# A key stage whose LayerNorm rows are made one tile earlier and partly turned by DMAs

## The chip, the cores and the metric

The kernel runs on one core of a Trainium2 chip. The time is that of one launch in device microseconds; of several runs the median is given. A core has five engines that work beside each other, each through its own list of instructions in order: TensorE (PE, with its weight loads PEld), VectorE (DVE), ScalarE (ACT), GpSimd (POOL) and SyncE (SP). In this kernel SP only issues DMAs. Engines wait for each other through semaphores.

## What is computed

The program is the forward and the backward pass of four residual blocks over 2048 rows of 512 numbers in bf16: attention, feed-forward, attention, feed-forward, with weights shared by the two blocks of a kind. Each block works on the LayerNorm of its input (mean taken off, divided by the standard deviation, no gain):

```python
x = x + _A_ref(_layernorm(x), A_wqkv, A_wo)
x = x + _B_ref(_layernorm(x), B_w_gate, B_w_up, B_w_down)
x = x + _A_ref(_layernorm(x), A_wqkv, A_wo)
x = x + _B_ref(_layernorm(x), B_w_gate, B_w_up, B_w_down)
```

`_A_ref` is linear attention with 32 heads of 16: q, k, v = x @ wqkv; phi(t) = (t + 1 if t > 0 else exp(t)) + 1e-6 is applied to q and k; kv is the sum over rows of phi(k) times v per head, z the sum of phi(k); the output is phi(q) @ kv divided by (phi(q) . z + 1e-6), times wo. `_B_ref` is (sigmoid(x @ w_gate) * (x @ w_up)) @ w_down with 1376 hidden units. The outputs are the result and, by the chain rule from grad_out, the gradients of x and of the five weights.

## The kernel before

The 2048 rows are 16 tiles of 128 (`st` 0 to 15). The change lies in the first key stage: `kq_fwd` with `l == 0`, the first 57 us. For every tile it makes the LayerNorm row h, turns it (the 512 features must lie on the partitions to be contracted), projects it to k and q, takes phi of both, and adds X = h^T phi(k) and z = sum of phi(k). The values are never projected: kv follows from X and the value weights at the stage's end.

For a tile the steps and engines are these:

- `ln.stats` (L512 to L520): mean and variance on DVE (bn_stats, bn_aggr), then three small operations on POOL (add of epsilon, power of -1/2, and the product "nmr").
- `ln.apply` (L528): one ACT operation writes h into `h_all`, which holds all 16 tiles. After each fourth tile a DMA saves four of them (L601).
- `stage_hT` (L608, L381): PE turns two tiles in eight 128x128 transposes into PSUM, ACT copies them into `hTst`, a buffer of four tiles with two copies. When four tiles are there, a DMA saves them for the backward pass (`store_hT`, L689).
- `proj` (L704): four matmuls per projection. After the first four projections they rotate over three PSUM tiles (`mm_tile`: t, t, y), so that a projection waits for the phi of the third one before it.
- phi: ACT takes the exponential (L732), DVE clamps both halves of k and q in one operation (L735), and then adds and takes the maximum once for k and once for q (L738). `save_phq` (L741) saves q's clamped half by DMA, out of a buffer with five copies.
- `X_some` (L712): three or four matmuls of X, for tiles at least two steps old; `z_add` (L726): POOL adds phi(k) of the tile two steps back to z, up to tile 11, and then splits the sum in two bf16 parts (L728, L729).

Tiles 0 to 3 go through `opening`, whose order is written out by hand in the string `OPEN`: s is stats, h apply, T transposes, k and q a projection with its exponential, a a clamp, p a phi, X and z the sums, each with its tile. Then a loop over `st` from 4 to 15 issues everything in program order, which the four computing engines keep (`manual_schedule`). In step `st` it projects k, (in odd steps) turns tiles st+1 and st+2, projects q (not in the last two steps, whose q comes later), applies tile st+3, does both phis, and takes the statistics of tile st+5, then z and X. The weights that later stages need are loaded from this loop: `k.late_loads` says after which step's `save_phq` SP issues which load. SP sends everything out in one queue, in order, and a DMA whose data are not ready holds up those behind it.

After the loop z and X are closed, kv and the product of kv with wo are formed, and the attention output and the feed-forward block follow tile by tile. There (`pair_front2`, L1020) the kernel already uses `dma_start_transpose` from on-chip memory to on-chip memory on tiles of 128x512.

Of the kernel before, what the change touches and what calls it, by code (L numbers as in the profile page):

```python
# [9 lines left out]
BF16 = mybir.dt.bfloat16  # L10
# [8 lines left out]
D = 512  # L19
# [46 lines left out]
def kernel(  # L66
# [81 lines left out]
    with tc.tile_pool(name="wfwd", bufs=1, reuse_waits="tile") as wfwd, ExitStack() as lctx, tc.manual_schedule(engines=EM):  # L148
        hctx, xctx = ExitStack(), ExitStack()
        wattn = xctx.enter_context(tc.tile_pool(name="wattn", bufs=1, side="right", reuse_waits="tile"))  # L150
        xin = xctx.enter_context(tc.tile_pool(name="xin", bufs=1, side="right", reuse_waits="tile"))
        hres = hctx.enter_context(tc.tile_pool(name="ln_hall", bufs=1, side="right", reuse_waits="tile"))
        x_bf = xin.tile([P, NST, D], BF16, name="x_bf")
        k.wqkv = wattn.tile([P, NDC, 3 * D], BF16, name="wqkv")
        wq_src = A_wqkv.rearrange("(c p) j -> p c j", p=P)
        for st in range(2):
            nc.sync.dma_start(out=x_bf[:, st, :], in_=x_in[rows(st), :])
        nc.sync.dma_start(out=k.wqkv[:, :, D:2 * D], in_=wq_src[:, :, D:2 * D])
        nc.sync.dma_start(out=x_bf[:, 2:NB, :], in_=dram_batch(x_in, 1, 2))
        nc.sync.dma_start(out=k.wqkv[:, :, 0:D], in_=wq_src[:, :, 0:D])  # L160
        for b in (1, 2):
            nc.sync.dma_start(out=x_bf[:, b * NB:(b + 1) * NB, :], in_=dram_batch(x_in, b))
        k.wo = wattn.tile([P, NDC, D], BF16, name="wo")

        def load_x(b):
            nc.sync.dma_start(out=x_bf[:, b * NB:(b + 1) * NB, :], in_=dram_batch(x_in, b))

        def load_attn():
            nc.sync.dma_start(out=k.wqkv[:, :, 2 * D:3 * D], in_=wq_src[:, :, 2 * D:3 * D])
            nc.sync.dma_start(out=k.wo[:], in_=A_wo.rearrange("(c p) j -> p c j", p=P))  # L170
        k.wg = wfwd.tile([P, NDC, FP], BF16, name="wg")
        k.wu = wfwd.tile([P, NDC, FP], BF16, name="wu")
        for w_sb in (k.wg, k.wu):
            nc.gpsimd.memset(w_sb[:, :, F:FP], 0.0)
        k.wd = wfwd.tile([P, NFC, D], BF16, name="wd")

        def load_wd():
            nc.sync.dma_start(out=k.wd[:, 0:NFC - 1, :],
                              in_=B_w_down[0:(NFC - 1) * P, :].rearrange("(c p) j -> p c j", p=P))
            for r0, r1 in ((0, 64), (64, FLAST)):  # L180
                nc.sync.dma_start(out=k.wd[r0:r1, NFC - 1, :],
                                  in_=B_w_down[(NFC - 1) * P + r0:(NFC - 1) * P + r1, :])
        k.late_loads = {
            0: lambda: load_x(3),
            3: lambda: nc.sync.dma_start(out=k.wg[:, :, 0:F], in_=B_w_gate.rearrange("(c p) j -> p c j", p=P)),
            7: lambda: nc.sync.dma_start(out=k.wu[:, :, 0:F], in_=B_w_up.rearrange("(c p) j -> p c j", p=P)),
            10: load_attn,
            13: load_wd,
        }

        k.lnres = dict(
            stg=lctx.enter_context(tc.tile_pool(name="ln_stg", bufs=2, reuse_waits="tile")),
            hT=lctx.enter_context(tc.tile_pool(name="ln_hT", bufs=2, reuse_waits="tile")),
            small=lctx.enter_context(tc.tile_pool(name="ln_small", bufs=6, reuse_waits="tile")),
        )
        lns = [FwdLNAll(k, hres, l, x_bf) if l % 2 == 0 else FwdLN(k, l) for l in range(4)]
        with tc.tile_pool(name="aq0", bufs=1, reuse_waits="tile") as aq:
            A = kq_fwd(k, aq, 0, lns[0], lns[1], x_bf)
            hctx.close()
            with tc.tile_pool(name="wt_stage", bufs=2, reuse_waits="tile") as wt_stage:  # L200
                fill = Fill(wT_groups_a(k, wt_stage), wT_dmas_a(k, wt_stage))
                A.tail(fill)
                ab_fwd(k, A, lns[1], fill, nxt=lns[2])
        with tc.tile_pool(name="aq2", bufs=1, reuse_waits="tile") as aq:
            ocur, bw = {}, {}
            k.g_in = g_in
            k.g_from_input = 3
            k.sv[3]["gbf"] = g_in

            def open_bwd():  # L210
                xctx.close()
                bw["wb"] = bctx.enter_context(tc.tile_pool(name="wbwd", bufs=1, side="right", reuse_waits="tile"))
                prectx = ExitStack()
                k.pre = dict(pool=prectx.enter_context(tc.tile_pool(name="pre", bufs=1, side="right",
                                                                    reuse_waits="tile")), close=prectx.close)
                bw["B3"] = BBwd(k, 3)

            A = kq_fwd(k, aq, 2, lns[2], lns[3])
            open_bwd()
            wb, B3 = bw["wb"], bw["B3"]  # L220

            def out_cb(st):
                if st % 2 == 0:
                    ocur["t"] = k.lnres["stg"].tile([P, 2, D], BF16, name="out0_t", tag="hstage")
                if st >= NST - 2:
                    nc.gpsimd.tensor_scalar(ocur["t"][:, st % 2, :], k.xs[st][:], 1.0, 0.0, ALU.mult, ALU.add)
                else:
                    nc.scalar.copy(ocur["t"][:, st % 2, :], k.xs[st][:])
                if st % 2 == 1:
                    nc.sync.dma_start(out=dram_batch(out0, st // 2, 2), in_=ocur["t"][:])  # L230

            fill = Fill(wT_groups_b(k, wb), wT_dmas_b(k))
            A.tail(fill)
            ab_fwd(k, A, lns[3], fill, out_cb=out_cb, bwd=B3)
# [337 lines left out]
class FwdLNAll:  # L572
# [47 lines left out]
XSTEP = 3  # L620
ZPOOL = 12
OPEN = """s1 h0 T0:t h1 T1 k0 k1 s2 s3 q0 s5 a0 h2 s4 s6 q1 T2:t h3 h5 q2 T3 a1 h4 pk0 k2 aq2 k3 T4:5
    pk1 pq2 pq0 pq1 ak2 ak3 pk2 pk3 h6 s7 q3 aq3 pq3 X2:0 X4:1 z1 s8""".split()
ZLAG = 2
QLATE = 2
WARM = 38


def kq_fwd(k, aq, l, ln, ln_next, x_src=None):
# [12 lines left out]
    with ExitStack() as ctx:  # L642
# [24 lines left out]
        def stage_hT(sts, evac, bank="ln"):  # L667
            st0 = sts[0]
            if st0 >= NST:
                return  # L670
            if st0 % NB == 0 or (st0 == 2 and ln.early):
                hTs["cur"] = stg.tile([P, 2, NDC, 2, P], BF16, name="hTst", bufs=2 if l == 0 else 3)
                hTq[st0 // NB] = hTs["cur"]
            put_hT(sts, evac, bank)
# [12 lines left out]
        def store_hT(b, a=0):  # L687
            hTs["cur"] = hTq.get(b, hTs["cur"])
            nc.sync.dma_start(out=sv["hT"][2 * b + a:2 * b + 2, :, :].rearrange("n p x -> p n x"),  # L689
                              in_=hTs["cur"][:, a:2, :, :, :].rearrange("p n c j t -> p n (c j t)"))  # L690

        def load_hT(b, half=(0, 1)):

            t = hTq[b] = hTq.get(b) or stg.tile([P, 2, NDC, 2, P], BF16, name="hTst", bufs=3)
            for a in half:
                nc.sync.dma_start_transpose(out=t[:, a, :, :, :].rearrange("p c j t -> p c (j t)"),
                                            in_=sv["h"][batch_rows(2 * b + a, 2), :])
                for j in range(2):
                    hTs[b * NB + 2 * a + j] = t[:, a, :, j, :]

        def proj(st, n, ps=None):
            ps = ps or mm_tile()
            for kc in range(NDC):
                nc.tensor.matmul(ps[:], lhsT=hTs[st][:, kc, :], rhs=k.wqkv[:, kc, n * D:(n + 1) * D],  # L704
                                 start=(kc == 0), stop=(kc == NDC - 1))
            return ps
# [33 lines left out]
        def save_phq(st, a):  # L740
            ins = nc.sync.dma_start(out=sv["phq"][rows(st), :], in_=a)  # L741
            if l == 0 and st in k.late_loads:
                with tc.issue_after(ins.ins):
                    k.late_loads[st]()
            if st % 2 == 1 and pieces:
                with tc.issue_after(ins.ins):
                    pieces.pop(0)()
# [80 lines left out]
        for st in range(NB if l == 0 else 0, NST):  # L828
# [11 lines left out]
            if l == 2 and st == 0:  # L840
                load_hT(1, (1,))
                stage_hT([2, 3], "vector")
            elif l == 2 and st == 2:
                hTs["cur"] = hTq[1]
                put_hT([4, 5], "vector")
            elif l == 0 and st % 2 == 1 and st >= 3:
                stage_hT([st + 1, st + 2], "scalar")
            if l == 2 or not both:
                clamp(ak, ek)
                phi_out(pk_all[:, st, :], ps_k, ak)  # L850
# [3 lines left out]
                    eq, aqt = qa_tiles()  # L854
                exp_to(eq, ps_q)
            if l == 0:
                ln.apply(st + 3)
                if both:
                    clamp(a_t[:], e_t[:])
                    phi_out(pk_all[:, st, :], ps_k, ak)  # L860
            elif st in (1, 2):
                ln.apply(NST - 3 + st)
# [3 lines left out]
                phi_out(A.pq(st), ps_q, aqt)  # L866
                save_phq(st, aqt)
            if l == 0:
                ln.stats(st + 5)
            store_pk(st)  # L870
            if l == 2 and st in (2, 5):
                load_hT(2 + st // NB)
# [1317 lines left out]
```

## Time and profile before

| | us |
|---|---|
| median of 3 runs | 1104.92 |
| lowest and highest run | 1104.79, 1106.0 |
| profiled execution | 1104.22 |
| its span | 1102.5 |
| step 4's k projection to the last X matmul | 17.73 to 56.3 |
| value weights, first read | 57.05 |
| gate weights, first read | 66.30 |

The span runs from the first to the last instruction of one profiled execution; the time of a run adds what lies around it. In a line of the timeline the first number is the start in us from the span's start, the second the length, then engine, line, operation, output and input; in brackets stands how long the engine was idle before it and what released it. A window's line gives busy time and, in brackets, the number of instructions of PE, PEld, DVE, ACT and POOL, then the granted PE clock, the busy share of the DMA engines and GB/s. "SPq" lines are DMA issues with SP's own time for them; the time from issue to landing is listed separately.

### The profile page before, as it was taken

How to read it: one execution, taken by the hardware profiler on the slowest of the kernel's cores; microseconds unless marked ns; L12 is line 12 of the kernel's file. 1: busy time of each engine (PE TensorE's matmuls, PEld its weight loads, DVE VectorE, ACT ScalarE, POOL GpSimd, SP SyncE). 2: the span in 40 equal slices, each digit the busy share in tenths (PEclk: the TensorE clock that was granted, in tenths of full speed). 3: DMA queues.
4: the chain of work that ended last, by engine and by line, in shares of the span. 5: the costliest groups of instructions: out<-in, count | busy, mean ns of one | idle time of the engine just before them, and what ended most of it. 6: DMA issues, size and time to landing. Idle time of an engine off the chain costs nothing. (4 is left out here: it accounts for less than half of the span.)

```text
span 1102.5 us, 19826 instructions
## 1 busy us (share of the span) xinstructions
PE 1076.6 (98%) x7255; PEld 660.9 (60%) x7356; DVE 719.1 (65%) x1257; ACT 484.9 (44%) x907; POOL 463.1 (42%) x631
## 2 busy tenths in 40 slices
PE   8999999999999999999999999999999999999998
PEld 4477777447777744445756556544447755555587
DVE  7798997878888667777965620067778946632221
ACT  6676555547555524444633441234346513420001
POOL 5637776435765447773101420048881102420000
PEclk9999999999999999999999999999999999999999
DMA  8948997796797688976899968898869999958997
GB/s 260 318 150 216 249 251 231 208 251 155 219 290 230 188 273 287 300 237 209 244 269 258 273 212 283 253 334 250 233 189 247 272 256 264 263 184 285 266 253 168
DMA packets 365330, 269.55 MB, mean 244 GB/s; under 512 B 132464, under 2 KB 339760, under 8 KB 365232
## 3 DMA queue, kind: packets, MB, share of 16 engines
q1 hardware_dynamic: 365232, 268.28, 85.3%
q8 instruction: 57, 0.93, 0.3%
q14 instruction: 41, 0.34, 0.1%
HBM read 122.62 MB, written 119.47 MB: 220 GB/s over the span
## 5 line engine op out<-in xcount | busy, mean ns | idle before, releaser
L1778 PE MATMUL p_ps<-p_set,p_a 128*128 128x384 bf16 (+2 forms) x1792 | 264.4, 303 | 1.5 <-DMA p_set<-sv_hdd 0.8
L1778 PEld LDWEIGHTS <-p_a 128*128 128x128 bf16 x1792 | 168.8, 96 | 85.0 <-PE p_ps L1778 1.0
L1469 POOL TENSOR_TENSOR dd<-dhb,ssd 128x512 bf16<-128x512 bf16 x84 | 97.0, 1158 | 102.9 <-ACT dhb L1467 96.3
L1468 DVE TENSOR_TENSOR dd<-dhh_ps,ssd 128x512 bf16<-128x512 f32 x85 | 57.2, 679 | 119.9 <-ACT dhb L1467 117.1
L1493 PE MATMUL dh_ps<-wuT,dd 128*128 128x512 bf16 (+1 forms) x339 | 128.5, 379 | 0.5
L1493 PE MATMUL dh_ps<-wgT,dd 128*128 128x512 bf16 (+1 forms) x329 | 124.7, 379 | 0.1
L1493 PEld LDWEIGHTS <-dd 128*128 128x128 bf16 x680 | 66.4, 98 | 79.6
L1152 POOL TENSOR_TENSOR ssd_t<-hhT,oms 128x512 bf16<-128x512 bf16 (+2 forms) x76 | 82.8, 1098 | 49.1 <-DVE hhT L1151 22.4
L1793 DVE TENSOR_TENSOR dw_stg<-p_ps,dw_stg 128x384 bf16<-128x384 f32 (+2 forms) x76 | 32.2, 438 | 105.6 <-PE p_ps L1778 96.7
L1467 ACT CAST dhb<-dhh_ps 128x512 bf16<-128x512 f32 x84 | 48.7, 589 | 115.4 <-PE dhh_ps L1461 108.1
L1133 PE MATMUL u_ps<-hT,wu 128*128 128x256 bf16 (+1 forms) x792 | 92.7, 261 | 1.2 <-DVE hhT L1151 1.0
L1133 PE MATMUL g_ps<-hT,wg 128*128 128x256 bf16 (+1 forms) x792 | 92.8, 261 | 0.7 <-DVE den L972 0.4
L1090 DVE STREAM_TRANSPOSE tr_stg<-dd 128x768 f32<-128x768 f32 (+1 forms) x62 | 86.8, 1435 | 1.5 <-DMA sv_hdd<-tr_stg 0.4
L1133 PEld LDWEIGHTS <-wg 128*128 128x128 bf16 x792 | 70.1, 98 | 17.0 <-issue 0.5
L1461 PE MATMUL dhh_ps<-gT,wdT 128*128 128x512 bf16 x299 | 76.9, 379 | 2.2 <-DVE dd L1468 1.5
L1168 PE MATMUL y_ps<-wd,hhT 128*128 128x512 bf16 (+1 forms) x337 | 77.7, 379 | 0.8
L1133 PEld LDWEIGHTS <-wu 128*128 128x128 bf16 x792 | 70.6, 98 | 9.0 <-issue 2.1
L1149 ACT ACTIVATE ssd_t<-g_ps 128x512 bf16<-128x512 f32 (+2 forms) x76 | 42.5, 559 | 63.2 <-PE g_ps L1133 60.6
L1795 ACT CAST dw_stg<-p_ps 128x384 bf16<-128x384 f32 (+2 forms) x76 | 28.1, 386 | 84.1 <-PE p_ps L1778 80.9
L1461 PEld LDWEIGHTS <-wdT 128*128 128x128 bf16 x352 | 34.2, 98 | 43.3 <-issue 3.5
L1151 DVE TENSOR_TENSOR hhT<-u_ps,ssd_t 128x512 bf16<-128x512 f32 (+2 forms) x76 | 47.2, 629 | 17.8 <-PE u_ps L1133 11.0
L1150 ACT ACTIVATE oms<-g_ps 128x512 bf16<-128x512 f32 (+2 forms) x96 | 53.7, 559 | 10.0 <-POOL ssd_t L1152 9.3
(256 smaller groups left out, 1879.8 us busy)
## 6 DMA issues: line engine op xcount, KB each, us to landing
sv_hdd<-tr_stg SPq DMA_DIRECT2D x72, 384.0 KB, 4.8
p_set<-sv_hdd SPq DMA_DIRECT2D x18, 1536.0 KB, 7.3
ssd<-sv_ssd SPq DMA_DIRECT2D x23, 768.0 KB, 5.2
sv_ssd<-ssd_t SPq DMA_DIRECT2D x61, 256.0 KB, 3.4
h_ld<-sv_h SPq DMA_DIRECT2D x30, 256.0 KB, 4.0
sv_hdl<-tr_stg SPq DMA_DIRECT2D x24, 256.0 KB, 5.1
p_a<-sv_h SPq DMA_DIRECT2D x12, 512.0 KB, 6.7
p_set<-sv_hdl SPq DMA_DIRECT2D x24, 256.0 KB, 5.0
```

The costliest lines, as they stand in the source:

```text
L1090: nc.vector.transpose(t[:, :, 0:n * P].bitcast(F32).rearrange("p q (a j) -> p q a j", a=2 * n), src.rearrange("p c x -> p (c x)").bitcast( ...
L1133: nc.tensor.matmul(ps[:, ci * n:(ci + 1) * n], lhsT=w_sb[:, kc, (c0 + ci) * P:(c0 + ci + 1) * P], rhs=hT[:, kc, (st % 2) * P:(st % 2) * P ...
L1150: nc.scalar.activation(oms, gv, ACT.Sigmoid, scale=-1.0)
L1151: nc.vector.tensor_tensor(hh, uv, ssd[:, :, 0, :], ALU.mult)
L1152: nc.gpsimd.tensor_tensor(ssd[:, :, 1, :], hh, oms, ALU.mult)
L1168: nc.tensor.matmul(y_ps[:], lhsT=h[0:r, fc, off:off + P], rhs=k.wd[0:r, fc, :], start=(fc == 0), stop=(fc == NFC - 1))
L1461: nc.tensor.matmul(ps[:], lhsT=k.wdT[:, jc, u * P:(u + 1) * P], rhs=self.gT[B][:, jc, :], start=(jc == 0), stop=(jc == NDC - 1))
L1467: nc.scalar.copy(dhb[:], ps[:])
L1468: nc.vector.tensor_tensor(self.dd[ng][:, 0, c, :], ps[:], self.ssd[ng][:, c, 0, :], ALU.mult)
L1469: nc.gpsimd.tensor_tensor(self.dd[ng][:, 1, c, :], dhb[:], self.ssd[ng][:, c, 1, :], ALU.mult)
L1493: nc.tensor.matmul(self.acc[j][:], lhsT=dd[0:r, a, c, j * P:(j + 1) * P], rhs=w[0:r, u, :], start=(u == 0 and a == 0), stop=(u == NFC - 1 ...
L1778: nc.tensor.matmul(ps[:, 0:w], lhsT=lhs[:, s, ic * P:(ic + 1) * P], rhs=rhs, start=(s == 0), stop=(s == NST - 1))
```

## The change

Three things change in this stage, and nothing elsewhere.

- Rows are made one tile earlier: `LEAD` is 4, so step `st` applies tile st+4 (was st+3) and takes the statistics of tile st+6 (was st+5). To start that, `OPEN` gets `h7` between `X2:0` and `X4:1`, and `s9` at its end.
- Tiles 8 to 15 are turned by a new `turn_hT`, called right after the apply: one `dma_start_transpose` on SP's queue for each tile, from `h_all` into the same `hTst` buffers. Tiles up to 7 are turned by PE as before (tiles 6 and 7 in step 5). The saves of the turned tiles 8 to 11 and 12 to 15 come at the end of steps 10 and 14.
- The late weight loads are cut: gate and up weights into four loads of 128 rows each, the value weights and wo into two halves each, w_down into pieces of four chunks. One is issued after step 2, one after each of steps 3 to 5, two after each step from 6 on until all are out, which is in step 11. Before, there were five places (steps 0, 3, 7, 10, 13). The load of x in step 0 stays.

```diff
-        def load_attn():
-            nc.sync.dma_start(out=k.wqkv[:, :, 2 * D:3 * D], in_=wq_src[:, :, 2 * D:3 * D])
-            nc.sync.dma_start(out=k.wo[:], in_=A_wo.rearrange("(c p) j -> p c j", p=P))
+        def load_v(half):
+            js = slice(2 * D + half * D // 2, 2 * D + (half + 1) * D // 2)
+            nc.sync.dma_start(out=k.wqkv[:, :, js], in_=wq_src[:, :, js])
+
+        def load_wo(half):
+            js = slice(half * D // 2, (half + 1) * D // 2)
+            nc.sync.dma_start(out=k.wo[:, :, js], in_=A_wo.rearrange("(c p) j -> p c j", p=P)[:, :, js])
...
-        def load_wd():
-            nc.sync.dma_start(out=k.wd[:, 0:NFC - 1, :],
-                              in_=B_w_down[0:(NFC - 1) * P, :].rearrange("(c p) j -> p c j", p=P))
+        def load_gu(t, src, c):
+            nc.sync.dma_start(out=t[:, c, 0:F], in_=src[c * P:(c + 1) * P, :])
+
+        def load_wd(c0, c1):
+            if c1 < NFC:
+                nc.sync.dma_start(out=k.wd[:, c0:c1, :],
+                                  in_=B_w_down[c0 * P:c1 * P, :].rearrange("(c p) j -> p c j", p=P))
+                return
+            load_wd(c0, NFC - 1)
             for r0, r1 in ((0, 64), (64, FLAST)):
                 nc.sync.dma_start(out=k.wd[r0:r1, NFC - 1, :],
                                   in_=B_w_down[(NFC - 1) * P + r0:(NFC - 1) * P + r1, :])
-        k.late_loads = {
-            0: lambda: load_x(3),
-            3: lambda: nc.sync.dma_start(out=k.wg[:, :, 0:F], in_=B_w_gate.rearrange("(c p) j -> p c j", p=P)),
-            7: lambda: nc.sync.dma_start(out=k.wu[:, :, 0:F], in_=B_w_up.rearrange("(c p) j -> p c j", p=P)),
-            10: load_attn,
-            13: load_wd,
-        }
+        parts = [lambda t=t, src=src, c=c: load_gu(t, src, c)
+                 for t, src in ((k.wg, B_w_gate), (k.wu, B_w_up)) for c in range(NDC)]
+        parts += [lambda f=f, i=i: f(i) for f in (load_v, load_wo) for i in range(2)]
+        parts += [lambda c=c: load_wd(c, min(c + 4, NFC)) for c in range(0, NFC, 4)]
+        k.late_loads = {0: [lambda: load_x(3)], 2: parts[0:1]}
+        for st in range(3, NST - QLATE):
+            n = 1 if st < 6 else 2 if st < 12 else 1
+            k.late_loads[st], parts[1:] = parts[1:1 + n], parts[1 + n:]
+        k.late_loads[NST - QLATE - 1] += parts[1:]
...
 OPEN = """s1 h0 T0:t h1 T1 k0 k1 s2 s3 q0 s5 a0 h2 s4 s6 q1 T2:t h3 h5 q2 T3 a1 h4 pk0 k2 aq2 k3 T4:5
-    pk1 pq2 pq0 pq1 ak2 ak3 pk2 pk3 h6 s7 q3 aq3 pq3 X2:0 X4:1 z1 s8""".split()
+    pk1 pq2 pq0 pq1 ak2 ak3 pk2 pk3 h6 s7 q3 aq3 pq3 X2:0 h7 X4:1 z1 s8 s9""".split()
...
+LEAD = 4
...
+        def turn_hT(st):
+
+            b, a, j = st // NB, st % NB // 2, st % 2
+            if st % NB == 0:
+                hTq[b] = stg.tile([P, 2, NDC, 2, P], BF16, name="hTst", bufs=2)
+            hTs[st] = hTq[b][:, a, :, j, :]
+            nc.sync.dma_start_transpose(out=hTs[st], in_=ln.h_all[:, st, :])
...
-            elif l == 0 and st % 2 == 1 and st >= 3:
-                stage_hT([st + 1, st + 2], "scalar")
+            elif l == 0 and st == 5:
+                stage_hT([6, 7], "scalar")
...
-                ln.apply(st + 3)
+                ln.apply(st + LEAD)
+                if LEAD + st < NST:
+                    turn_hT(st + LEAD)
...
-                ln.stats(st + 5)
+                ln.stats(st + LEAD + 2)
+                if st in (10, 14):
+                    store_hT(st // NB)
```

More of the change, by code (lines that the diff above doesn't have):

```diff
@@ L743, in save_phq @@
                 with tc.issue_after(ins.ins):
-                    k.late_loads[st]()
+                    for load in k.late_loads[st]:
+                        load()
             if st % 2 == 1 and pieces:
```

## The prediction

> **What bounds the kernel now.** I read the page first, then busy time by window, then the timelines of the first 60 us, engine by engine, because the change touches nothing later. On the page:
>
> ```profile
> PE 1076.6 (98%) x7255; PEld 660.9 (60%) x7356; DVE 719.1 (65%) x1257; ACT 484.9 (44%) x907; POOL 463.1 (42%) x631
> ```
>
> TensorE is the limit over the whole span, so a delay in the first stage should arrive at the end almost undiminished. The windows of the stage look similar (columns PE, PEld, DVE, ACT, POOL, clock, DMA share, GB/s), but here PE is not alone: DVE is at 85% and the DMA engines are full.
>
> ```profile
> 26.00:32.00 6.00, 5.73 (x33) 2.77 (x32) 5.13 (x11) 4.59 (x7) 4.84 (x9) 1.00 0.78 283
> 32.00:38.00 6.00, 5.78 (x33) 2.77 (x32) 5.14 (x11) 4.59 (x7) 4.85 (x9) 1.00 0.95 298
> 38.00:44.00 6.00, 5.73 (x32) 2.82 (x32) 4.72 (x10) 4.59 (x7) 4.84 (x9) 1.00 1.08 364
> ```
>
> So I looked at what releases each projection (timeline, steps 8 to 10; L704 is a projection, L608 the transposes the change removes):
>
> ```profile
> 31.31 1.02 PE L704 MATMUL t_mm<-wqkv,hTst 128*128 128x512 bf16 x4 [0.22 <-DVE pk_all L738]
> 32.37 0.60 ACT L732 ACTIVATE e_t<-t_mm 128x512 bf16<-128x512 f32 x1 [0.65 <-PE t_mm L704]
> 33.00 0.43 DVE L735 TENSOR_SCALAR e_t<-e_t 128x1024 bf16<-128x1024 bf16 x1 [0.26 <-ACT e_t L732]
> 33.46 0.69 DVE L738 SCALAR_TENSOR_TENSOR pk_all<-t_mm,e_t 128x512 bf16<-128x512 f32 x1
> 33.68 0.61 PE L608 MATMUL hT_tp<-ident,h_all 128*128 128x128 bf16 x8
> 34.21 1.02 PE L704 MATMUL t_mm<-wqkv,hTst 128*128 128x512 bf16 x4
> 37.17 1.02 PE L704 MATMUL y_mm<-wqkv,hTst 128*128 128x512 bf16 x4 [0.22 <-DVE pk_all L738]
> ```
>
> Call the query projection of step s q_s. It writes the PSUM tile that k_(s-1) used, so it waits for phi_k(s-1) on DVE. The loop is q_8 31.31, exponential 32.37, clamp 33.00, phi_k 33.46 to 34.15, q_9 34.21: 2.90 us a step, on four engines in turn. The transposes stand from 33.68 to 34.21, where PE would wait for phi_k anyway (34.15 plus 0.05 of hand-over). q_10 follows after 2.96, because exp of step 9 starts at 35.32 behind the 1.01 us copy of the turned tiles, where q_9's end allowed 35.27.
>
> The opening (ACT, then POOL):
>
> ```profile
> 19.65 0.60 ACT L732 ACTIVATE e_t<-y_mm 128x512 bf16<-128x512 f32 x1 [0.27 <-PE y_mm L704]
> 20.41 0.81 ACT L528 ACTIVATE h_all<-x_bf,ln_nmr,rstd_all 128x512 bf16<-128x512 bf16 x1 [0.16 <-POOL ln_nmr L520]
> ...
> 20.11 0.27 POOL L520 TENSOR_SCALAR ln_nmr<-ln_mv,rstd_all 128x1 f32<-128x1 f32 x1
> 22.61 0.27 POOL L520 TENSOR_SCALAR ln_nmr<-ln_mv,rstd_all 128x1 f32<-128x1 f32 x1
> ```
>
> h7 (the row of tile 7) runs the moment its statistics are ready, at 20.38; those of tile 8 are ready at 22.88. Both exponentials of step 4 are ahead of h7 on ACT.
>
> The end of the loop, where tile statistics run out (POOL, then DVE):
>
> ```profile
> 43.01 4.92 POOL L726 TENSOR_TENSOR z_acc<-z_acc,pk_all 128x512 f32<-128x512 f32 x4
> 48.02 0.62 POOL L728 TENSOR_SCALAR X_sb<-z_acc 128x512 bf16<-128x512 f32 x1
> ...
> 44.72 0.96 DVE L735 TENSOR_SCALAR e_t<-e_t 128x1024 bf16<-128x1024 bf16 x1 [1.15 <-ACT e_t L732]
> 48.15 0.77 DVE L735 TENSOR_SCALAR e_t<-e_t 128x1024 bf16<-128x1024 bf16 x1 [1.15 <-ACT e_t L732]
> ```
>
> Four sums of z run back to back, and a clamp that falls into one takes 0.96 in place of 0.43: it ends about 0.27 after the POOL operation does. That made q_13 come 3.43 after q_12.
>
> **The change part by part.** Times are of the profiled execution: span 1102.5, run 1104.22, 0.70 under the median of 1104.92.
>
> *Transposes and copies of tiles 8 to 15.* 32 PE transposes (four times 0.53) and four ACT copies (1.01) go. If PE were the limit, 4 x 0.53 = 2.1 would be gained, and 0.05 for each copy: -2.3 in all. By the loop above the next thing late is phi_k, at the same moment; only the copies' 0.06 is left, before q_8, q_10 and q_12: -0.18. I take -0.18: the steps of 2.96 never had transposes in them, and still PE waits 0.22 on phi_k there.
>
> *h7 into the opening, ahead of k4's and q4's exponentials.* Its statistics start on DVE at 18.14 behind unchanged work, so h7 still starts at 20.41, and ACT stands from 18.03. exp k4 goes from 18.79 to 21.21, exp q4 from 19.65 to 21.74, ending 22.34. Clamp 4 starts at 22.37 (was 20.75, 1.02 long because of z1 on POOL at 20.34 to 21.49; now 0.43), phi_k4 22.83 to 23.52, q_5 at 23.57: was 22.55, +1.02. The statistics of tile 9, moved ahead of clamp 4, take 0.9 of DVE, hidden while DVE waits for exp q4.
>
> *h8 in step 4.* It waits for its statistics (22.88; about 23.1 if clamp 4 holds POOL, as POOL's 0.57 power takes 0.71 beside a clamp in later steps). Behind it stand exp k5 (+0.80), the copy of tiles 6 and 7, which stays (+0.51), and exp q5 (+0.89): 25.35, where it was 23.61. q_6 comes 1.84 later, at 27.19: +1.74 in all, of which 0.2 is the POOL wait (bounds 1.5 to 1.74). After that each step takes 2.90 and nothing pays it back.
>
> *POOL's run of sums.* Statistics end at step 9, not 10, so five z sums, not four, stand in a row from q_9 + 5.84, 1.25 apart. Clamp 11, at q_9 + 7.49, meets the second (+0.60). Clamp 12, at q_9 + 10.98, meets the fifth, which starts 0.13 ahead of it; before, the 0.62 us cast stood there, now a 1.16 us sum (+0.86). Before, only 0.53 of this lay ahead of q_13. Net +0.93; bounds -0.53 (no meeting) and +1.5 (two waits of 1.0). I take +0.93, as the same distance of 0.13 was a meeting before (48.02 and 48.15).
>
> *Eight transposes by SP.* The same move, 128x512 on chip, is in the trace later:
>
> ```profile
> L1020 SPq DMA_TRANSPOSE pqnT<-pqnstage x20: 1189/1254/2275, 94.3 to 348.6; - x20
> ...
> DMA to landing us min/median/max: 2.4/2.5/4.5
> ```
>
> Each holds SP for 1.25 and waits for its row from ACT (about q_s + 2.4). Its tile is needed by k_(s+4), 7.8 later. Behind it on SP wait phq saves, weight pieces and stores; in steps 6 to 9 that is 1.25 + 0.34 + 2 x 0.5 + 0.28 (stores of h, hT, pk shared out) = 2.87 of 2.90. Landing by the nearest rows: 2.5, or 3.9 (median of the 128 KB phq saves in this very stage, longest 7.3). All are under 7.8, so 0; bounds 0 and +4 (rival 2). The hT store, now at steps 10 and 14, and the phq tiles (five buffers, refilled 12 us on) wait on SP only.
>
> *Weight pieces.* Two loads of 1376 KB, two of 512 and the 1376 KB of wd, seven issues, become 17, the last in step 11 and not 13. They are read from 57 on (values) and 66 on (gate); no engine waits for a DMA between 10 and 50, so 0 either way, SP's share counted above.
>
> Sum: -0.18 + 1.74 + 0.93 = +2.5: 1106.7 for the profiled execution, 1107.4 against the median.
>
> **Rivals.**
> 1. *No meeting on POOL.* The distance of 0.13 is small; with opening +1.74, copies -0.18 and the old 0.53 gone it is +1.0, 1105.9 (1105.5 to 1106.6). Against: the distances are the old ones, moved one step.
> 2. *Turned tiles come late.* From 20 to 50 the DMA engines moved 9.6 MB at 320 GB/s, at best 400, so 12 could pass; added are 1.4 (wd, earlier) and 1 to 2 (eight tiles read and written), so up to 1 MB or 2.5 us of backlog, beside an SP with no slack. It decides once issue plus landing exceeds 7.8; a landing of 7.3 with SP 2 late gives +1.5, with the backlog +4: 1108.4 to 1111.5. Against: 2.5 us landings, and slack grows to over 8 for tiles 13 to 15.
>  The Trainium skill (DMA: Bandwidth & Descriptors, Anatomy of one DMA) puts one transfer at about 2.0 us plus bytes over 436 GB/s, and its Rules for kernel authors ask for 1 MiB or more. By that the eight gate and up pieces would cost 22 us of transfer against 10 for the two loads, 12 more, and this rival would be certain, near 1111. The stage moved its 128 KB saves and 512 KB stores at 320 GB/s, so here fixed costs overlap, and I keep rows over rule.
> 3. *Faster: the loop shortens and pays the opening back.* If q_s could start ahead of phi_k's end, PE's own work, 4 x 0.86 + 7 x 0.215 = 4.95 a pair, or DVE's, about 5.15, would set the pair in place of 5.86: four pairs, -2.8. With +1.74 and no meeting (-0.53) that is -1.6, 1103.3; with less opening delay 1102. It decides if pairs take under 5.4. For it: PE and ACT get room. Against: the three 0.22 waits on phi_k.
>
> **How the numbers follow.** This kernel's measurement tells about 0.2%, 2.2 us, from no change: 1102.7 and 1107.1. The forecast, 1107.4 (own range 1106.6 to 1108.4), has 0.44, of which 0.30 is over 1107.1. Rival 1 has 0.18, all within. Rival 2 has 0.24, all slower. Rival 3 has 0.14: 0.08 faster, 0.06 within. So slower 0.54, within 0.38, faster 0.08. The range goes from 1104.0 (0.1 below, rival 3) to 1110.5 (0.08 above, rival 2).
>
> **What would show it.** Right: ACT idle about 2.4 before the h7 row, released by POOL; q_5 near 23.6 and q_6 near 27; steps of 2.90 with PE waiting about 0.5 on phi_k where the transposes stood; two long clamps, in steps 11 and 12; q_13 near 48.9 and not 46.46. Wrong: a projection waiting for a DMA of hTst (rival 2), pairs well under 5.8 (rival 3), clamps of 0.43 throughout (rival 1).

## The result, and the profile after

The changed kernel takes 1117.92 us (median of four runs, 1117.31 to 1121.25) beside 1104.86 us for the kernel before on the same chip: a ratio of 1.0124, 95% interval 1.0112 to 1.0136, so 1.2% slower, 13.1 us. The profiled execution took 1117.49 with a span of 1115.8, that is 13.3 more span than before.

The page of the changed kernel hides it almost wholly, because most of the loss is in the first 70 us of 1116:

```profile
PE 1078.2 (97%) x7223; PEld 660.2 (59%) x7324; DVE 718.8 (64%) x1257; ACT 480.8 (43%) x903; POOL 462.4 (41%) x631
```

PE is as busy as before, in a longer span. Windows of ten microseconds of the changed kernel show where the room is (columns: window, length, busy time of PE, PEld, DVE, ACT, POOL, granted clock, DMA share, GB/s; a DMA share near or over 1 is read here as full):

```profile
30.00:40.00 10.00, 9.22 (x40) 3.98 (x41) 8.71 (x18) 6.25 (x11) 8.13 (x14) 1.00 1.05 261
40.00:50.00 10.00, 7.69 (x34) 3.14 (x34) 6.07 (x10) 4.91 (x9) 8.81 (x10) 1.00 1.17 292
50.00:60.00 10.00, 3.75 (x15) 1.37 (x14) 2.70 (x5) 1.09 (x2) 0.00 (x0) 0.75 1.09 305
```

From 50 to 60 PE works 3.75 of 10 us, the mean clock falls to 0.75, and from 54 to 58 all engines but SP stand while DMAs run. PE's timeline in the changed kernel names the wait (in brackets: the idle time before the group, and what ended it):

```profile
23.58 1.02 PE L725 MATMUL t_mm<-wqkv,hTst 128*128 128x512 bf16 x4 [1.67 <-DVE pk_all L759]
27.17 1.02 PE L725 MATMUL t_mm<-wqkv,hTst 128*128 128x512 bf16 x4 [0.65 <-DVE pk_all L759]
...
41.65 1.02 PE L725 MATMUL t_mm<-wqkv,hTst 128*128 128x512 bf16 x4 [0.36 <-DVE pk_all L759]
...
44.84 1.04 PE L725 MATMUL y_mm<-wqkv,hTst 128*128 128x512 bf16 x4 [1.52 <-DMA hTst<-h_all]
...
47.82 1.04 PE L725 MATMUL t_mm<-wqkv,hTst 128*128 128x512 bf16 x4 [0.43 <-DMA hTst<-h_all]
...
50.56 1.03 PE L725 MATMUL t_mm<-wqkv,hTst 128*128 128x512 bf16 x4
...
58.48 1.89 PE L725 MATMUL t_mm<-wqkv,hTst 128*128 128x512 bf16 x4 [6.25 <-DMA hTst<-h_all]
60.16 1.81 PE L733 MATMUL X_ps<-pk_all,h_all 128*128 128x512 bf16 x4
...
67.64 1.06 PE L928 MATMUL kv_ps<-X_sb,wqkv 128*128 128x128 bf16 x16
```

In the kernel before, k_15 and the first product into `kv_ps` were these:

```profile
49.69 1.03 PE L704 MATMUL t_mm<-wqkv,hTst 128*128 128x512 bf16 x4
...
57.26 1.06 PE L902 MATMUL kv_ps<-X_sb,wqkv 128*128 128x128 bf16 x16
```

The first three lines of the changed kernel are q_5, q_6 and q_11, where the forecast put them. Then the key projections of tiles 12, 13 and 15 wait for DMAs of `hTst`, the turned rows. k_15 starts at 58.48, where it was 49.69; its four matmuls take 1.89 in place of 1.03, and the X products behind it 1.81 in place of 1.03, at the lower clock. As a marker of the stage's end I use the first product into `kv_ps`: 57.3 before, 67.6 after, +10.3. The other 3 us come later.

SP's timeline in the changed kernel shows why the turns are late (L720 is a turn, L762 a phq save, L182 and L170 weight pieces):

```profile
24.08 1.30 SPq L720 DMA_TRANSPOSE hTst<-h_all  x1
...
36.28 0.53 SPq L762 DMA_DIRECT2D sv_phq<-e_t  x1
36.85 0.94 SPq L182 DMA_DIRECT2D wu<-in_B_w_up_dram  x2
37.89 0.40 SPq L774 DMA_DIRECT2D sv_pk<-pk_all  x1
38.39 2.39 SPq L720 DMA_TRANSPOSE hTst<-h_all  x1
40.88 0.53 SPq L762 DMA_DIRECT2D sv_phq<-e_t  x1
41.46 1.05 SPq L170 DMA_DIRECT2D wqkv<-in_A_wqkv_dram  x2
42.61 1.61 SPq L720 DMA_TRANSPOSE hTst<-h_all  x1
...
50.23 2.09 SPq L720 DMA_TRANSPOSE hTst<-h_all  x1
```

The turn of tile 8 is issued at 24.08, that of tile 15 at 50.23: 3.74 us a tile, where the loop had 2.90. SP works almost without a gap (0.05 to 0.1 between issues). The turns take it 1.30 to 2.39 and a phq save 0.53, where the forecast had 1.25, from the same move later in the kernel before, and 0.34. The query for that one source line gives the landings:

```profile
L720 SPq DMA_TRANSPOSE hTst<-h_all x8: 1304/1810/2389, 24.1 to 50.2; - x8
...
DMA to landing us min/median/max: 2.5/5.2/8.2
```

The last turn is issued 6.2 us after its row is ready (44.01) and lands 8.2 us later. Two saves of 512 KB, of `hTst` and of h, are issued just ahead of it, at 49.15 and 49.76.

### The profile page after: what moved, and what is told of

It is laid out like the page before. It is cut to its first block, busy times and chain, and to the rows that moved or that the text cites. A ratio compares the mean times of both kernels' runs of the same rounds, so it can differ in the third digit from the quotient of the medians.

```text
span 1115.8 us, 19784 instructions
## 1 busy us (share of the span) xinstructions
PE 1078.2 (97%) x7223; PEld 660.2 (59%) x7324; DVE 718.8 (64%) x1257; ACT 480.8 (43%) x903; POOL 462.4 (41%) x631
## 5 line engine op out<-in xcount | busy, mean ns | idle before, releaser
L528 POOL TENSOR_TENSOR rstd_all<-rstd_all,neghalf 128x1 f32<-128x1 f32 x64 | 37.4, 584 | 52.4 <-DVE rstd_all L527 47.6
```

## The experiments

The theory from these profiles: SP's queue and the DMA engines, loaded by turns and weight pieces together, make the turns late (T1). Rivals: the turns alone are too slow (T2), the pieces alone do harm (T3), or the opening and the sums on POOL cost more than the forecast said (T4). "Marker" is the start of the first `kv_ps` product, 57.3 before and 67.6 after. Ratios are to the kernel before, run on the same chip.

**The turns undone.** Tiles 8 to 15 are turned by PE and ACT again; opening, lead and pieces stay.

```diff
-            elif l == 0 and st == 5:
-                stage_hT([6, 7], "scalar")
+            elif l == 0 and st % 2 == 1 and st >= 3:
+                stage_hT([st + 1, st + 2], "scalar")
...
-                if LEAD + st < NST:
-                    turn_hT(st + LEAD)
```

> The changed kernel with tiles 8 to 15 turned by TensorE and ACT again; the earlier rows, the reordered opening and the weight pieces stay. Theory Q (the turned tiles are late because SP's queue is overfull; opening and POOL cost as in the prediction): no wait on a DMA, q_13 near 48.9 us, 1107 to 1108, so about 10 us less than the changed kernel. Rival P (the weight pieces or the opening do most of the harm by themselves): 1110 or more.

Measured: 1107.25, ratio 1.0014 [1.0004, 1.0023]; marker 59.8, which is 2.5 over before, the sum of the forecast. The DMA waits are gone, q_5 comes at 23.64, q_6 at 27.23, and PE's timeline of this kernel shows q_12 and q_13 late by the meetings on POOL:

```profile
41.85 1.02 PE L725 MATMUL t_mm<-wqkv,hTst 128*128 128x512 bf16 x4
...
45.27 1.02 PE L725 MATMUL t_mm<-wqkv,hTst 128*128 128x512 bf16 x4 [0.67 <-DVE pk_all L759]
...
49.03 1.02 PE L725 MATMUL y_mm<-wqkv,hTst 128*128 128x512 bf16 x4 [0.78 <-DVE pk_all L759]
```

Steps of 3.42 and 3.76 in place of 2.90. The forecast's two meetings on POOL are in the lines of POOL and DVE of this kernel:

```profile
41.82 6.15 POOL L747 TENSOR_TENSOR z_acc<-z_acc,pk_all 128x512 f32<-128x512 f32 x5
46.96 1.29 DVE L756 TENSOR_SCALAR e_t<-e_t 128x1024 bf16<-128x1024 bf16 x1 [1.15 <-ACT e_t L753]
```

The fifth sum runs from 46.81 to 47.96 and the clamp ends at 48.25. So T4 falls, and 7.8 of the stage's 10.3 us hang on the turns. k_14 came at 50.75 here and at 50.56 in the changed kernel: its waits of 1.52 and 0.43 only took the place of these long steps. The 7.8 are the wait for tile 15, 6.2, and 1.6 of slow clock after it.

**The weights moved behind the turns.**

```diff
-        k.late_loads = {0: [lambda: load_x(3)], 2: parts[0:1]}
-        for st in range(3, NST - QLATE):
...
+        k.late_loads = {0: [lambda: load_x(3)], 12: [load_w["v"], load_w["wo"]],
+                        13: [load_w["wg"], load_w["wu"], load_w["wd"]]}
```

> The changed kernel with the DMA turns kept, but no weight load between steps 1 and 11: values and wo after step 12, gate, up and down after step 13, in whole loads. Theory Q: SP's cycle falls to about 2.5 us a step, each turn is issued within 1 us of its row and lands in 2.5 to 4, no projection waits for hTst, 1106.5 to 1108 (the opening and POOL terms stay). Rival X (a turn on chip is too slow here whatever stands beside it): the waits of k_12 to k_15 stay, over 1112.

Measured: marker 59.8, no wait on `hTst`; the source query for the turns:

```profile
L723 SPq DMA_TRANSPOSE hTst<-h_all x8: 1196/1604/1833, 24.2 to 45.3; - x8
...
DMA to landing us min/median/max: 2.5/3.2/3.9
```

Tile 15 is turned at 45.3 and not 50.2, and lands within 3.9. T2 falls: without weights beside them the eight turns are in time. The total, 1113.1, ratio 1.0059 [1.0040, 1.0078], holds a side effect of this kernel: PE works 0.66 of the 4 us from 68 to 72. The gate weights are not the cause: they are issued at 51.50 and land 9.3 later, long before. SP is held from 54.46 to 62.15 by the last pieces of w_down, so the save of `pk_all` goes out at 62.73 and lands 8.3 later, at 71.03. ACT's first copy into `wt_st`, a tile made after the stage's tiles are given up, stands 3.90 until 71.18, and PE waits for that copy. That the copy waits for this save is argued from the times; no run separates it.

**The old whole loads at their old places**, turns by DMA.

```diff
+        k.late_loads = {0: [lambda: load_x(3)], 3: [load_w["wg"]], 7: [load_w["wu"]],
+                        10: [load_w["v"], load_w["wo"]], 13: [load_w["wd"]]}
```

> The changed kernel with the DMA turns, but the weights in the old whole loads at the old places (3, 7, 10, 13). The same bytes beside the turns up to step 10 in 4 issues and not 12, and w_down later. Theory Q (issues count): SP keeps up to within 2 us, 1107 to 1109. Rival D (bytes on the DMA engines count): turns behind a 1376 KB load land late all the same, some projections wait, 1109 to 1114.

Measured: 1115.43, ratio 1.0086 [1.0071, 1.0101]; marker 63.2. PE's timeline here:

```profile
55.65 1.04 PE L728 MATMUL t_mm<-wqkv,hTst 128*128 128x512 bf16 x4 [2.82 <-DMA hTst<-h_all]
```

With four loads in place of the first 12 pieces, so with the bytes in few issues, the turns are late too (the longest landing is 8.1), by 3.4 us of the marker over the kernel with late weights.

**The issues without the bytes**: as with the late weights, and 17 loads of 4 KB to unused tiles where the pieces were.

```diff
+        for i, st in enumerate((2, 3, 4, 5, 6, 6, 7, 7, 8, 8, 9, 9, 10, 10, 11, 11, 11)):
+            k.late_loads.setdefault(st, []).append(lambda i=i: tiny(i))
```

> As e2, and 17 loads of 4 KB each into unused tiles where the changed kernel issues its 17 weight pieces: SP's issues without the bytes. Theory Q: SP's cycle is again over 2.9 us a step, the last turns are issued 3 to 6 us after their rows and projections wait for hTst; 1110 to 1117. Rival D: as e2, 1106.5 to 1108.

Measured: marker 60.8, with one wait of 1.00 on `hTst`: SP's time for 17 more issues is worth 1.0 us. The total of 1120.02, ratio 1.0124 [1.0108, 1.0139], again holds the late save (here it lands at 74.5, and PE waits 5.80 until 75.26; the gate weights had landed at 64.2). Issues 1.0, bytes in whole loads 3.4, pieces that are both 7.8: the two parts do not add up to the whole. Three things are in the difference that no run separates: 1.6 of the 7.8 is slow clock, which neither part has; the first pieces of w_down are issued ahead of the last turn in the changed kernel (48.07) and 5.8 behind it with the whole loads; and the turns themselves took SP longer, 14.5 for all eight against 11.8 here.

**The pieces alone**: the kernel before with only its weight loads replaced by the pieces.

```diff
-        def load_attn():
...
+        def load_gu(t, src, c):
+            nc.sync.dma_start(out=t[:, c, 0:F], in_=src[c * P:(c + 1) * P, :])
```

> The kernel before with the weight pieces alone. With tiles turned by TensorE nothing in the loop waits for a DMA, so the first product of kv stays at 57.3 us and the time within 1 us of before. Rival: small pieces cost DMA time that someone waits for, 1107 or more.

Measured: 1104.39 beside 1104.42, ratio 0.9997 [0.9987, 1.0006]; marker 57.6. T3 falls.

**The weights ahead of the turns**: the changed kernel, with gate and up weights loaded whole behind the first loads, the rest after steps 12 and 13.

```diff
+        load_w["wg"]()
+        load_w["wu"]()
+        k.late_loads = {0: [lambda: load_x(3)], 12: [load_w["v"], load_w["wo"]], 13: [load_w["wd"]]}
```

> The changed kernel with the gate and up weights loaded whole right behind the first loads of x and wqkv, where SP and the DMA engines are idle, values and wo after step 12, w_down after step 13. If the weight loads beside the turns are what delays them, no projection waits for hTst, the first product of kv stands at 59.8 us as in e1 and e2, and no later wait for the gate weights arises as in e2: 2.5 us over before. Rival: the turns wait all the same (over 61), or the early loads delay x and the opening.

Measured: 1109.1, ratio 1.0044 [1.0029, 1.0059]; marker 59.5 and no wait on `hTst`. T1 holds on both sides, weights early or late. The marker is 2.3 over before, the whole 4.7; the rest arises later.

**Only the DMA turns**: the same with the old opening and three tiles' lead.

```diff
-LEAD = 4
+LEAD = 3
...
-    pk1 pq2 pq0 pq1 ak2 ak3 pk2 pk3 h6 s7 q3 aq3 pq3 X2:0 h7 X4:1 z1 s8 s9""".split()
+    pk1 pq2 pq0 pq1 ak2 ak3 pk2 pk3 h6 s7 q3 aq3 pq3 X2:0 X4:1 z1 s8""".split()
```

> As e7, but rows three tiles ahead and the opening as before: only the DMA turns of tiles 8 to 15 remain of the change, with the weights out of their way. If the reordered opening and the earlier end of the statistics are the other 2.5 us, the first product of kv stands at 57.0 to 57.4 (57.3 before) and the time is within 1 us of before. A turn then has 4.9 us from its issue to its use. Rival: that is too short, projections wait for hTst by 1 to 3 us in all.

Measured: 1108.73, ratio 1.0037 [1.0022, 1.0052]; marker 58.9. q_5 is at 22.54 and q_6 at 25.43, as in the kernel before: the opening's delay belongs to the fourth tile of lead. Now the turns are short of time: the wait for tile 15 is 1.68. q_13 is at 46.29, level with before (46.46) and 2.4 ahead of the kernel with early weights (48.73); the late tile 15 takes most of that back, so the marker is 0.6 ahead of early weights and 1.7 behind before. Part of the wait may be the value and wo loads: the last turn is issued at 46.40, they follow at 48.08 and 48.70, and it lands after 4.9, where with four tiles' lead it landed after 3.4, with the first of them issued as it landed. Lead and loads were not separated.

**A shorter run of sums**, on the kernel with PE turns: POOL adds up 8 tiles, not 12.

```diff
-ZPOOL = 12
+ZPOOL = 8
```

> As e1 (tiles turned by TensorE), and POOL sums z only up to tile 7; TensorE adds the other eight at the end of the loop, 4 more matmuls of 0.215. If the run of five POOL sums causes the long steps (q_11 to q_12 3.42 and q_12 to q_13 3.76 us in e1), both are 2.9 to 3.0 here, q_13 about 1.3 us earlier than in e1, and the first product of kv about 0.4 us earlier (59.4). Rival: the long steps have another cause and stay.

Measured: 1107.87, ratio 1.0028 [1.0017, 1.0040]; marker 60.4. Step 12 got longer (4.13), step 13 normal (2.90). The timeline of this kernel:

```profile
42.90 0.62 POOL L749 TENSOR_SCALAR X_sb<-z_acc 128x512 bf16<-128x512 f32 x1
43.60 1.15 POOL L750 TENSOR_TENSOR X_sb<-z_acc,X_sb 128x512 bf16<-128x512 f32 x1
43.73 1.30 DVE L756 TENSOR_SCALAR e_t<-e_t 128x1024 bf16<-128x1024 bf16 x1 [1.51 <-ACT e_t L753]
...
47.50 0.43 DVE L756 TENSOR_SCALAR e_t<-e_t 128x1024 bf16<-128x1024 bf16 x1 [1.15 <-ACT e_t L753]
```

I had expected both steps normal. The meeting was not removed but moved: the clamp at 43.73 now falls behind the subtraction that ends the sums, and waits for its end (44.75). The clamp at 47.50, with POOL silent, takes 0.43. So a clamp that starts beside a running POOL operation ends 0.3 after it, here and with the run of five sums (48.25 after 47.96), and is short where POOL is silent; that a shorter run avoids the meeting is not shown.

**Four PSUM banks.** PE's transposes had been costed at nothing, since a query projection waits for phi_k through the rotation over three banks. With the transposes gone, the bank `ln` is free. The kernel with only the DMA turns, and that with early weights and four tiles' lead, get it as a fourth:

```diff
             nm = "gugu"[cnt[0]] if cnt[0] < 4 else "tty"[(cnt[0] - 4) % 3]
+            if l == 0 and cnt[0] >= 12:
+                nm = ("y", "t", "ln", "t")[cnt[0] % 4]
```

> Three tiles' lead, DMA turns, weights whole and early or late, as in e8_lead3; from the thirteenth projection on the projections' outputs take four PSUM banks in turn (y, t, ln, t) in place of three, since the ln bank is no longer used for turning tiles. Theory (the transposes that PE lost were worth nothing because a q projection waits for phi_k of the tile before, through the rotation over three banks): with four banks that wait is gone, the step of the loop falls from 2.90 us towards PE's own work of 12 matmuls x 0.216 = 2.6 us from tile 6 on, and the stage marker (first kv_ps matmul) comes at 58.9 - 9 x 0.3 = 56.2 if the turned tiles are in time. They were short by 1 to 2 us with three tiles' lead already, so 1 us or more of that should come back as waits on hTst: 56.5 to 58.5. Rival (VectorE, 2.52 us busy of each 2.90, or POOL sets the step): the step stays at 2.90 and the marker at 58.9; time 1108.7.

> e7_early_weights (four tiles' lead, DMA turns, gate and up weights loaded whole at the start, the rest after step 12) with the same rotation over four PSUM banks. Theory: q_5 at 23.5 and q_6 at 27.1 as before the rotation; then steps of 2.6 to 2.65 in place of 2.90 until tile 11; no wait, or less than 1 us, on a turned tile; stage marker 59.5 - 8 x 0.28 = 57.2, time 1106.9. Rival (VectorE or POOL sets the step): steps of 2.90, marker 59.5, time 1109.1.

Measured: with three tiles' lead 1110.51, ratio 1.0043 [1.0030, 1.0056], marker 58.1, and PE waits 0.36, 1.49, 0.24 and 1.62 on turned tiles; with four 1106.84, ratio 1.0010 [0.9999, 1.0020], marker 55.6, one wait of 0.30. PE's timeline with four tiles' lead:

```profile
27.07 1.02 PE L731 MATMUL t_mm<-wqkv,hTst 128*128 128x512 bf16 x4 [0.64 <-DVE pk_all L765]
27.93 0.81 PE L739 MATMUL X_ps<-pk_all,h_all 128*128 128x512 bf16 x3
28.58 1.03 PE L731 MATMUL ln_mm<-wqkv,hTst 128*128 128x512 bf16 x4
29.44 1.03 PE L731 MATMUL t_mm<-wqkv,hTst 128*128 128x512 bf16 x4
30.31 1.03 PE L739 MATMUL X_ps<-pk_all,h_all 128*128 128x512 bf16 x4
31.17 1.03 PE L731 MATMUL y_mm<-wqkv,hTst 128*128 128x512 bf16 x4
32.03 1.03 PE L731 MATMUL t_mm<-wqkv,hTst 128*128 128x512 bf16 x4
```

q_6 27.07, q_7 29.44, q_8 32.03: 4.96 a pair, without a wait, PE's own work (the forecast's rival 3 had worked out 4.95). The rotation was the chain's closing link. The stage is now 1.6 us shorter than in the kernel before although its opening costs 1.74 more, and still the whole is not faster. The marker is better than the 57.2 that I had expected because the meetings on POOL stop counting too: clamps of 0.78 to 0.94 are still there, but q_6 to q_13 takes 17.27, seven steps of 2.37 to 2.59, where with three banks it took 21.66 with the two long steps in it.

**The opening back as it was**, four banks, with step 6 making two rows to get the fourth tile of lead.

```diff
-                ln.apply(st + LEAD)
-                if LEAD + st < NST:
-                    turn_hT(st + LEAD)
+                for t in lead_tiles(st):
+                    ln.apply(t)
+                    if 8 <= t < NST:
+                        turn_hT(t)
```

> e10_four_banks_lead4 with the kernel before's opening (three tiles' lead, no h7 and s9 in it); step 6 makes the LayerNorm rows and the turns of tiles 9 and 10, and from there the lead is four tiles. Theory: the cost of the opening (+1.02 at q_5, +1.74 at q_6) is that of two more h rows in front of tile 4's and 5's exponentials, so q_5 is back at 22.6 and q_6 at 25.5; the steps are 2.5 but for step 6 or 7, which carries one row more (ScalarE 0.81, VectorE 0.69 + 0.18) and may be up to 0.9 longer; less than 1 us of waits on turned tiles 8 and 9, which have three tiles' lead; stage marker 55.6 - 1.7 + 0.3 to 0.9 = 54.2 to 54.8. If what comes after the stage is as in e10, the time is 1106.84 - 1 = 1105.8, which is not told from that of the kernel before. Rival (the turns at three tiles' lead are as late as in e9, where 3.7 us of PE's waits were on them): marker 55.6 or later.

Measured: 1107.38, ratio 1.0018 [1.0009, 1.0028]; marker 55.7. q_5 and q_6 are back (22.28, 25.18), but the wait for tile 15 is 1.72 and the marker no earlier: the rival. What the opening gave, the turns took; the value load is issued at 45.56 here, while the last turn (42.60, landing after 5.5) is in flight.

**What arises after the stage.** Against the runs on the same chip, the kernels whose projections read DMA-turned tiles lose 2.2 to 3.8 us more than their marker says (the change itself 2.7, whole loads 3.5, early weights 2.4, only turns 2.6, four banks 3.4 and 2.2, the last 3.8); those that read PE-turned tiles between -1.3 and +0.3. The two with late weights are left aside. This sets medians of many runs beside the marker of one profiled execution, and the medians are known to 1 to 2 us. Span and marker of the same execution part the two kinds less well: 1.3 to 5.2 with DMA turns (1.3 with only turns), 1.4 in both kernels with PE turns and four tiles' lead, -0.5 to +0.4 where only pieces or spare transfers were added. So how much of the loss belongs to DMA-turned tiles is not settled. I tried whether the turns' traffic does it: in the kernel before, SP turns the same eight rows into a tile that is free then and that nobody reads, or copies them there untransposed.

```diff
                 ln.apply(st + 3)
+                if 8 <= st + 3 < NST:
+                    spare(st + 3)
```

> The kernel before with one addition: at steps 5 to 12 SP also turns the rows of tiles 8 to 15 by DMA, into a tile that is free then and that nobody reads (the MT tile, written over later); PE and ScalarE go on turning the tiles that are used. Open is what becomes of time after the stage: in the profiles the kernels with DMA turns lose 2.3 to 3.8 us more in all than at the stage marker (first kv_ps matmul), those with PE turns and the pieces alone do not. Theory A (eight DMA turns change how later transfers land, by themselves): the marker at 57.3 to 58.3, the time 2 to 4 us over that of the kernel before plus the marker's shift, so 1107.5 to 1110. Theory B (the loss comes from the time at which later work meets later loads, or from where tiles lie, not from the turns): the time is that of the kernel before plus the marker's shift, 1105.2 to 1106.2.

> As e12_spare_turns, but each spare transfer is a plain DMA copy of the same 128 KB from the same row tile to the same place, no transpose. Theory A (the small packets of the transposing DMA): marker and time as in the kernel before, 1105 to 1106, while e12 is slower. Rival (eight more transfers of any kind on SP's queue do it): as slow as e12. If e12 is not slower, this should not be either.

Measured: 1105.29, ratio 0.9995 [0.9986, 1.0004], marker 57.6; and 1104.90, ratio 0.9992 [0.9983, 1.0001], marker 57.3. Theory A falls for the kernel before: turns that nobody waits for cost it nothing that shows, at once or later. Matching ScalarE's instructions one by one with those of before, four banks with four tiles' lead is 2.0 ahead at 217 us, 0.9 ahead at 373, 0.4 behind at 426, 1.3 behind at 584 and 1.7 behind at 1071. The same places cost the kernel with PE turns time too: 0.5 more at 426 than at 400, and 1.6 more by 584. Two of the places are late landings of reloads: POOL's wait for `ssd` ahead of 421.5 is 4.7 in the kernel with only the turns, and the same wait is 2.7 before; near 1068 PE waits 1.7 for `sv_dq` in the one with four banks and four tiles' lead, where before it waited 0.4. Why these land later is open.

## Why the prediction was wrong, point by point

- **The step that failed is "Eight transposes by SP: all are under 7.8, so 0".** Three of its inputs had been taken as constants and are not. SP's time was "2.87 of 2.90" with 1.25 a turn and 0.34 a save; beside pieces and saves the turns took 1.30 to 2.39, a save 0.53, and the cycle 3.74, so lateness grew tile by tile to 6.2 us; the 0.05 to 0.1 between issues was in no term either. The landing was taken as 2.5 or 3.9; it was 5.2 in the middle and 8.2 at the end. And the slack was a sum of both: 6.2 + 8.2 less 7.8 is 6.6, near the 6.25 us that PE waited. The words "SP with no slack" stood in rival 2; a queue that is 99% full with the lowest known durations should have been costed with the higher ones.
- **Rival 2 was the right mechanism and too small.** It had +1.5 to +4 and ended at 1111.5 (its lower end of 1108.4 should be 1108.9, 1107.4 and 1.5); the turns cost 7.8 in the stage. Its reckoning of the DMA engines assumed that 400 GB/s could pass. From 20 to 50 us before moved 9.6 MB at a share of 0.97, after 8.0 MB (266 GB/s) at 1.01, and the kernel with PE turns, which has the same pieces, 319 GB/s at 1.00: with turns among them, full engines carried less. In the first 60 us 5088 packets were under 512 bytes, before 672. The 1.6 us of slow clock behind the long wait was in no step.
- **"I keep rows over rule" held for the pieces and did not save the forecast.** The forecast worked the 12 us of transfer out from the fit of the Trainium skill (DMA: Bandwidth & Descriptors, Anatomy of one DMA), which that section gives for DMAs issued by GpSimd; here SP issues them. Alone the pieces cost nothing (0.9997). The same page, in its section on latency and other measured facts, gives a DMA transpose 261 GB/s in one case measured with a strided middle dimension and 350 to 400 for a contiguous one; that is the sentence I should have weighed. The 261 to 292 GB/s of the full windows here stand near it, though other transfers are among theirs.
- **Right: transposes and copies worth -0.18.** With the opening and lead of the change, the marker is at 59.83 with PE turns, and at 59.78 and 59.53 with DMA turns that are in time (weights late, weights early, so moved as well): the removal is worth 0.05 to 0.30. The reason given, the wait for phi_k through three banks, is shown by the four-bank kernels.
- **Right: h7 and h8 in the opening, +1.02 and +1.74.** q_5 at 23.58 (forecast 23.57), q_6 at 27.17 (27.19), q_11 at 41.65; ACT idles 2.20 before h7 with POOL as releaser, forecast "about 2.4".
- **Right: POOL's run of five sums.** With PE turns q_13 came at 49.03, forecast 48.9; the two steps were 0.52 and 0.86 too long, forecast 0.60 and 0.86, and the clamps met the second and the fifth sum as the forecast has it. In the changed kernel itself these meetings are hidden behind the DMA waits.
- **Weight pieces 0**: right alone, wrong beside the turns; "SP's share counted above" is where the bytes were lost sight of.
- **The sum of +2.5 for the rest of the change** stands at the stage's marker (59.83 with PE turns, 57.26 before). In the time of that kernel it is +1.3, ratio 1.0014 [1.0004, 1.0023]. Of the changed kernel's loss, 7.8 more in the stage are explained by the runs, 2.7 after it are not.

## What to carry to other kernels

When a transfer replaces an engine's work, its deadline has to be checked against issue time plus landing at the load of that stage: durations taken from a quiet stage are lower bounds, and a queue with no slack turns each excess into lateness that adds up step by step. Off-path work is removed in vain while a buffer rotation closes the loop; look first at which buffer the waiting instruction rewrites, and what the removal frees. One long wait at the end of a stage can cost more than its length: here the short waits took the place of others, and the long one took the clock with it.

## What the runs showed of the hardware

- **The clock falls in one long wait.** Windows of the changed kernel:

```profile
52.00:56.00 4.00, 0.23 (x2) 0.00 (x0) 1.25 (x3) 0.27 (x1) 0.00 (x0) 0.86 0.99 349
56.00:60.00 4.00, 1.52 (x4) 0.58 (x5) 0.00 (x0) 0.00 (x0) 0.00 (x0) 0.50 1.22 262
60.00:64.00 4.00, 4.00 (x16) 1.62 (x15) 1.07 (x3) 1.18 (x2) 0.00 (x0) 0.78 0.89 326
```

 After 6.25 us without matmuls the granted clock is 0.50 and the next eight matmuls take 3.7 in place of 2.06. In the kernel with the whole loads, a wait of 2.82 left its matmuls at 1.04 for four, the full clock. In the kernel with late weights, after a wait of 3.35 that ends at 71.82, the first sixteen matmuls took 1.05 and the next sixteen 1.84, with a clock of 0.50 from 74 to 76. This agrees with the Trainium skill (TensorE: Matmul & The Clock Gate, Part 1: The HAM clock gate), where the clock is halved after an idle window of about 3.4 us.
- **Transposing DMAs beside other traffic lower what the engines move.** The kernel before with spare turns, then with spare copies of the same rows, from 40 to 50 us:

```profile
40.00:50.00 10.00, 9.34 (x56) 4.53 (x53) 7.17 (x13) 7.09 (x11) 8.91 (x12) 1.00 1.02 263
```

```profile
40.00:50.00 10.00, 9.35 (x52) 4.42 (x50) 7.17 (x13) 7.13 (x11) 8.97 (x11) 1.00 1.07 373
```

 Both have full DMA engines; 263 GB/s with transposes, 373 with copies. Over 20 to 50 us the gap is smaller: 276 at a share of 0.98, 319 at 0.96. A spare turn took SP 1.19 to 3.40 us, a spare copy 0.47 to 1.26. The copies landed no sooner than the turns, 6.5 in the middle against 5.3 (longest 8.8 and 8.7), so a late landing here is a matter of the load and not of transposing alone.
- **An issue takes SP longer right behind another.** A phq save took 0.32 to 0.34 standing alone in the kernel before. In the kernel with tiny issues it took 0.38 to 0.40 when issued 0.1 behind a 4 KB load, and 0.51 to 0.54 when issued 0.1 behind a turn; in the changed kernel 0.52 to 0.54 behind a turn, once 1.21. With tiny issues the DMA share from 40 to 50 us is 0.56, so the 0.5 behind a turn does not need full DMA engines.
- **A bf16 clamp of 128x1024 waits for the end of a running POOL operation**: 0.43 alone, 1.29 and 1.30 in the two cases above, ending 0.3 after the POOL operation. The Trainium skill (SBUF — State Buffer, SBUF: two separate sides) has it as an exclusive lock of the port pair that the two engines share; the trace agrees.
